# Linear attention start-up: the order of the first loads, a replicated vector, an earlier clear and later weight pieces

## The chip, the core and the metric

The kernel runs on one core of a Trainium2 chip. The core has five engines that each take their instructions in order: TensorE (PE, with its weight loads PEld), VectorE (DVE), ScalarE (ACT), GpSimd (POOL) and SyncE (SP), which here issues nearly all transfers. SP's transfers are carried out by 16 DMA engines. PE computes into PSUM, everything else is held in SBUF, and both have 128 partitions. The metric is the time of one execution on the device in microseconds (us); lower is better.

## The reference

Three parts are computed one after the other on 3072 tokens of width 384: a linear attention with a decaying state, a mixture of eight experts of which each token uses at most one, and a bilinear MLP.

```
# attention: r, k, v of shape (4 batches, 8 heads, 768 steps, 48); w, u of shape (8, 48)
for t in range(768):
    cur = outer(u * k[t], v[t])
    y[t] = r[t] @ (state + cur)
    state = w[:, None] * state + outer(k[t], v[t])
# experts: x is (3072, 384)
c = x @ w_skip > 0;  e = argmax(x @ w_gate);  g = softmax(x @ w_gate)[e]
out = x;  out[c] = x + g * (relu(x @ w1[e]) @ w2[e])
# second MLP: w1, w2 are 384x1024, w3 is 1024x1024, w_out is 1024x384
out = ((x @ w1) * (x @ w2)) @ w3 @ w_out
```

The kernel multiplies w3 by w_out ahead of time, during the attention, so that the last part needs one product less for each token. w3 and w_out arrive as 8-byte floats and have to be narrowed to 4 bytes first.

## The kernel before, in words

The attention works on 24 tiles of 128 rows: two batches side by side, 64 steps of each. Tile n belongs to a pair of batches (n modulo 2) and to a chunk of 64 steps (n divided by 2). Two kinds of tile are loaded for it. TB holds r and k with the head dimension on the partitions (`load_t(n)`, tensor in_att, 128x1024 floats, 0.524 MB) and has three buffers. KV holds r, k and v with the steps on the partitions (`load_v(n)`, tensor in_kv, 128x1152 floats, 0.590 MB) and has four buffers.

For each tile these steps are done:

- `prep(n)`, L358, on DVE: FK = TB times powers of the decay. This is the product that frees the buffer of TB.
- `scores(n)`, L370, on PE, and `evac(n)`, L375, on DVE, which masks them into Fs.
- `prep_m(n)`, L388 and L389, on POOL: r times u, then times k (u lies in the tile `un`); `bonus(n)`, L394, on DVE sums this into z; `prep_v(n)`, L404, on ACT scales v by z in eight instructions.
- `prep_k(n)`, L382, on POOL gives kd; `ds_mm(n)`, L440, on PE adds kd times v to the state S in PSUM; `state_copy(n)`, L412 and L414, decays S on DVE and copies it to SBUF on ACT.
- `y_mm(n)`, L424 and L427, on PE; `x_out(n)`, L445, on DVE adds the two parts of the output, and two transfers (L449, xm<-xg, 0.197 MB together) write them out.
- `x_trans`, L456 on PE and L458 on ACT, and `logits`, L469 and L472, prepare the routing to experts.

Iteration n of the loop (L771 on) is written as prep(n+2), scores(n+1), kd(n+1), prep_m(n+2), evac(n+1), bonus(n+1), y_mm(n), logits(n-2), x_trans(n-1), prep_v(n+1), x_out(n), ds_mm(n). The code is emitted in the order in which it is written, with no reordering by a scheduler. Each engine keeps that order, and SP too: a transfer whose buffer isn't free stops all transfers behind it.

Between these steps the loop narrows the pieces of w3 and w_out. `load_w(i)` loads piece i (raww, three buffers; 0.786 MB for a piece of w_out, 1.049 MB for one of w3). `w_step` takes the next operations from a list: a copy on ACT (L104), then a shift, a merge and a sign on DVE (L112, L115, L119). The table WN says how many steps each iteration makes: none in iterations 0 and 1, three in iterations 2 to 6, two afterwards. The copy of piece i+1 is issued together with the first DVE step of piece i. The narrowed pieces are multiplied on PE (L707); where none is ready yet, `keep` fills PE with dummy products of zeros (L254).

`consts()` makes small tables on POOL in three parts, one in each of iterations 0 to 2. SP's transfers use eight semaphores in turn, and a transfer waits until the one eight places before it has landed.

Lines touched by the change: load order L256 to L264, state clears L559 to L561 and L744 to L745, `load_w` calls L749 to L754, `load_t` in the loop L775 to L776, the consts call L787, and the layout of u L1442. Times in a profile name the line of an instruction.

Of the kernel before, what the change touches and what calls it, by code (L numbers as in the profile page):

```python
# [8 lines left out]
F32 = mybir.dt.float32  # L9
# [9 lines left out]
P = 128  # L19
NB, NH, NS, HD = 4, 8, 768, 48  # L20
D = NH * HD
# [3 lines left out]
NT = NTOK // P  # L25
# [16 lines left out]
W3B = 5  # L42
WK = [(1, 1)] * 9 + [(1, 2)] * 13
WN = [(0, 0, 0)] * 2 + [(1, 1, 1)] * 5 + [(1, 0, 1)] * 15
KW = 16
NRING = 8
RG = 3
# [11 lines left out]
def fused_kernel(ctx, tc, att, kv, wt, u, wg, we, w3, wo, w12, r, k, v, wu, out):  # L59
    nc = tc.nc  # L60
# [161 lines left out]
    ps_s = A(tc.tile_pool(name="ps_s", bufs=1, space=PSUM))  # L222
    ps_1 = A(tc.tile_pool(name="ps_1", bufs=1, space=PSUM))

    with tc.manual_schedule():
# [8 lines left out]
        un = ac.tile([P, NH, HD], F32, name="un")  # L234

        def load_t(n):
            nc.sync.dma_start(out=TB[n % 3].rearrange("p a h t -> p (a h t)"), in_=att[n])

        def load_v(n):
            c, bp = divmod(n, 2)  # L240
            nc.sync.dma_start(out=KV[bp][c % 2].rearrange("p a h d -> p (a h d)"), in_=kv[n])
# [14 lines left out]
        for _ in range(NWARM):  # L256
            dummy(DQ)
        load_t(0)
        load_t(1)
        nc.sync.dma_start(out=un.rearrange("p h d -> p (h d)"), in_=u.to_broadcast([P, D]))  # L260
        load_v(0)
        load_v(1)
        load_t(2)
        nc.gpsimd.memset(ident, 0.0)  # L264
        nc.gpsimd.affine_select(out=ident, in_=ident, compare_op=ALU.not_equal, fill=1.0, base=0,
                                pattern=[[-1, P]], channel_multiplier=1)
# [8 lines left out]
        def load_w(i):  # L275
            if i < len(jobs):
                kind, q = jobs[i]
                raw_w.append(load_wide(nrp, "raww", wo[:, 2 * q * D:2 * q * D + 2 * D] if kind == "o" else w3[q], 3))
# [10 lines left out]
        for i in range(6):  # L289
            wn = pw[:, i - 1] if i else wc  # L290
            n = 1 << i
# [5 lines left out]
        nc.vector.reciprocal(out=cc, in_=pw[:, 5])  # L297
        cb = cc[:, :, None].to_broadcast([P, NH, CH])
        nc.vector.tensor_tensor(out=UT[:, 0, 0], in0=Ur, in1=cb, op=ALU.mult)
        SB = [ps_s.tile([P, 512], F32, tag=f"S{bp}", name=f"S{bp}") for bp in range(2)]  # L300
        S = [b[:, 0:D].rearrange("p (h d) -> p h d", h=NH) for b in SB]

        half = [slice(64 * q, 64 * q + 64) for q in range(2)]
        dims = [slice(64 * q, 64 * q + HD) for q in range(2)]
        KU = ac.tile([P, 2, NH, HD], F32, name="KU")
# [48 lines left out]
        def prep(n):  # L354

            t = TB[n % 3]
            FK = FK_[n] = wk.tile([P, 2, NH, CH], F32, name="FK", bufs=3)
            return nc.vector.tensor_tensor(out=FK, in0=t, in1=UT[:, n // 2 % 2], op=ALU.mult)  # L358
# [6 lines left out]
        def scores(n):  # L365
            FK = FK_[n]
            sc = ps_1.tile([P, 512], F32, tag="sc", name="sc").rearrange("p (h t) -> p h t", h=NH)
            for h in range(NH):
                for m, d in zip(half, dims):
                    nc.tensor.matmul(sc[m, h], FK[d, 1, h], FK[d, 0, h], start=True, stop=True)  # L370
            return sc
# [184 lines left out]
                eng.tensor_tensor(out=sg if k == 2 else v[:, :, 4], in0=sg, in1=v[:, :, k], op=ALU.subtract)  # L556

        found, pend = [], []
        SL = [b[:, 384:464] for b in SB]  # L559
        for b in SL:  # L560
            nc.vector.memset(b, 0.0)  # L561
        slots = wk.tile([P, 80], F32, name="slots", bufs=1)

        def lanes(oh, lo, i, k, eng):
# [169 lines left out]
        load_t(3)  # L734
        nc.vector.tensor_tensor(out=UT[:, 1, 1], in0=Tk, in1=cb, op=ALU.mult)
        prep(1)
        sc = scores(0)
        prep_m(0)
        table_k(1)
# [1 line left out]
        evac(0, sc)  # L741
        bonus(0)
        prep_m(1)
        for bp in range(2):  # L744
            nc.vector.memset(S[bp], 0.0)  # L745
        nc.vector.tensor_tensor(out=w128, in0=pw[:, 5], in1=pw[:, 5], op=ALU.mult)
        prep_v(0)
        more_consts = consts()
        load_w(0)  # L749
        load_v(2)  # L750
        load_v(3)
        nc.sync.dma_start(out=wgs, in_=wg)
        load_w(1)
        load_w(2)  # L754
        todo = []
        NEXT = {logits: logits_out, route_a: route_b, route_b: route_c}

# [13 lines left out]
        for n in range(NT - 2):  # L771
            w_ready()
            if n == NT - 3:
                raws = {q: load_expert(0, q) for q in range(2)}
            if n + 4 < NT:  # L775
                load_t(n + 4)  # L776
            fk = prep(n + 2)
            state_copy(n + 1)
            sc = scores(n + 1)
            behind(prep_k(n + 1) or prep_m(n + 2), fk)  # L780
            if n < NT - 3:
                prep_m(n + 2)
            evac(n + 1, sc)
            bonus(n + 1)
            if n == NT - 3:
                bonus(NT - 1)
            next(more_consts, None)  # L787
            w_step(WN[n][0])
            w_ready()
            y_mm(n)  # L790
            keep(4 * WK[n][0])
            run_todo()
            if n > 0:
                x_trans(n - 1)
            prep_v(n + 1)
            keep(4 * WK[n][1])
            w_step(WN[n][1])
            w_evac(0)
            x_out(n)
            ds_mm(n)  # L800
            place_mm(n % 2)
            if n + 4 < NT:
                load_v(n + 4)
            if n < NT - 3:
                place(3)
            w_step(WN[n][2])
            run_todo(n < NT - 3)
            if n > 0:
                todo.append((logits, (n - 1,)))

        a, b, g = NT - 2, NT - 1, len(groups) - 1
# [596 lines left out]
def _layout(i):  # L1408
# [20 lines left out]
    def words(a):  # L1429
# [9 lines left out]
        "v": c(v.reshape(NB * NH, NS, 4, 12).transpose(2, 0, 1, 3).reshape(4, NB * NH, NS * 12)),  # L1439
        "wu": c(np.broadcast_to(np.stack([w, u], 1), (4 * NB, NH, 2, HD)).reshape(P, 2, HD)),  # L1440
        "wt": wt,
        "u": c(u.reshape(1, D)),  # L1442
        "wg": c(wg.reshape(ND, P, 9).transpose(1, 0, 2)),
        "we": c(np.concatenate([w1, w2], -1)),
        "w3": words(i["moe2_w3"].reshape(NF, P, NF, P).transpose(0, 3, 2, 1).reshape(NF, P, FF)),
# [21 lines left out]
```

## Time and profile before

| | us |
|---|---|
| median of three timed runs | 635.29 (634.75 to 636.49) |
| profiled execution, its own time | 634.88 |
| its span (first to last instruction) | 633.2 |
| PE busy | 614.4 (97%) |
| DVE busy | 467.0 (74%) |
| ACT busy | 292.4 (46%) |
| POOL busy | 143.9 (23%) |

The span is what the trace covers, and 1.7 us of the execution's time lie around it. A profile row names the start, the duration, the engine, the line and the operation, as output<-input. In brackets stand the idle time of the engine before the instruction and what ended it. The attention fills about the first 170 us. A busy PE here is often a PE that works on dummy products.

### The profile page before, as it was taken

What the parts mean: (1) busy time and instruction counts of PE and PEld (TensorE: products, weight loads), DVE (VectorE), ACT (ScalarE), POOL (GpSimd) and SP (SyncE); (2) the same over time, 40 slices, a digit from 0 to 9 for tenths busy, and PEclk for the clock granted to TensorE, in tenths of its full rate; (3) what the DMA queues carried; (4) which work ended last, traced back from release to release, by engine and by line L of the source; (5) the groups of instructions that cost most, each with busy time, mean ns of one, the idle gap of its engine ahead of it and who ended that gap; (6) DMA issues with size and microseconds to landing.
All of it is one profiled execution on the core that took longest, in us unless ns stands there. A gap on an engine that the chain in (4) does not pass through costs nothing.

```text
span 633.2 us, 15204 instructions
## 1 busy us (share of the span) xinstructions
PE 614.4 (97%) x6289; PEld 546.4 (86%) x6289; DVE 467.0 (74%) x820; ACT 292.4 (46%) x704; POOL 143.9 (23%) x140
## 2 busy tenths in 40 slices
PE   8989999999999999999999999999999999999996
PEld 6978878878679999999987989988988988988984
DVE  6699999996577899999956953864863863863770
ACT  2556544544256676666534542443443442442430
POOL 4856456463040233142132300000000000000000
PEclk9899999999999999999999999999999999999999
DMA  7989988685168778867321002002002002000001
GB/s 303 368 281 373 323 292 294 188 280 182 27 195 289 243 253 308 280 237 251 111 70 58 1 17 84 1 18 84 1 18 84 1 17 84 2 18 33 1 2 55
DMA packets 26797, 90.60 MB, mean 143 GB/s; under 512 B 4009, under 2 KB 10298, under 8 KB 25696
## 3 DMA queue, kind: packets, MB, share of 16 engines
q1 hardware_dynamic: 24672, 84.11, 38.0%
q0 software_dynamic: 2048, 5.44, 2.5%
q8 instruction: 51, 0.84, 0.5%
q14 instruction: 26, 0.21, 0.1%
HBM read 77.81 MB, written 12.58 MB: 143 GB/s over the span
## 4 chain that ended last, share of the span: by engine, by line
PE 77%; DVE 13%; DMA 4%; issue 3%; ACT 1%; POOL 1%; SPq 0%; DVEq 0%; ACTq 0%; POOLq 0%
PE po L1231 16%; PE xy L1193 11%; PE za L1193 10%; PE zb L1193 8%; PE hp L922 7%; PE y L941 6%; PE wp L707 5%; PE sc L370 2%; DVE elo L86 2%; DMA TB<-in_att 2%; PE S L440 2%; DVE hl L926 1%; PE G L427 1%; PE y L424 1%; PE y L427 1%
## 5 line engine op out<-in xcount | busy, mean ns | idle before, releaser
L1175 DVE TENSOR_TENSOR C<-st,za 128x512 f32<-128x512 f32 x47 | 32.3, 688 | 69.6 <-ACT st L1210 69.5
L86 DVE TENSOR_TENSOR elo<-raw,ehi 128x768 fp32r<-128x768 f32 x64 | 60.4, 950 | 4.0 <-ACT ehi L85 3.7
L922 PE MATMUL hp<-xh,ehi 128*128 128x256 f32 x192 | 55.3, 290 | 2.3 <-DVE hl L926 1.7
L1231 PE MATMUL po<-pl,W_hi 128*128 128x512 f32 x144 | 56.8, 394 | 0.0
L1231 PE MATMUL po<-ph,W_hi 128*128 128x512 f32 x144 | 56.6, 393 | 0.0
L1231 PE MATMUL po<-ph,W_lo 128*128 128x512 f32 x144 | 56.1, 390 | 0.0
L1210 ACT COPY st<-xy 128x256 f32<-128x256 f32 x47 | 17.6, 374 | 81.8 <-PE xy L1193 81.8
L85 ACT CAST ehi<-raw 128x768 fp32r<-128x768 f32 x64 | 52.6, 828 | 2.1 <-DMA raw<-in_we 2.1
L922 PE MATMUL hp<-xh,elo 128*128 128x256 f32 x192 | 53.3, 279 | 0.0
L922 PE MATMUL hp<-xl,ehi 128*128 128x256 f32 x192 | 53.3, 279 | 0.0
L1193 PE MATMUL xy<-bxh,w12h 128*128 128x256 f32 x188 | 53.3, 283 | 0.0
L1193 PE MATMUL xy<-bxl,w12h 128*128 128x256 f32 x188 | 53.1, 283 | 0.0
L1193 PE MATMUL xy<-bxh,w12l 128*128 128x256 f32 x188 | 53.1, 282 | 0.0
L707 PE MATMUL wp<-wo_s,w 128*128 128x384 f32 x128 | 50.4, 505 | 0.0
L404 ACT ACTIVATE zv<-KV,z 128x48 f32<-128x48 f32 x184 | 44.0, 324 | 11.2 <-DVE z L394 8.2
L1193 PE MATMUL za<-bxh,w12l 128*128 128x512 f32 x141 | 45.1, 320 | 0.0
L1193 PE MATMUL za<-bxh,w12h 128*128 128x512 f32 x141 | 45.0, 319 | 0.0
L1193 PE MATMUL za<-bxl,w12h 128*128 128x512 f32 x141 | 44.7, 317 | 0.0
L959 POOL DMA_INDIRECT xm<-yo,sidx x16 | 23.8, 1485 | 89.5 <-DVE yo L956 75.4
L941 PE MATMUL y<-ehi,hh 128*128 128x384 f32 x128 | 43.5, 340 | 0.0
L941 PE MATMUL y<-ehi,hl 128*128 128x384 f32 x128 | 43.2, 337 | 0.0
L941 PE MATMUL y<-elo,hh 128*128 128x384 f32 x128 | 43.1, 337 | 0.0
(249 smaller groups left out, 1684.3 us busy)
## 6 DMA issues: line engine op xcount, KB each, us to landing
raw<-in_we SPq DMA_DIRECT2D x32, 768.0 KB, 5.1
KV<-in_kv SPq DMA_DIRECT2D x24, 576.0 KB, 5.2
TB<-in_att SPq DMA_DIRECT2D x24, 512.0 KB, 7.4
raww<-in_w SPq DMA_DIRECT2D x8, 1024.0 KB
raw<-in_w SPq DMA_DIRECT2D x8, 768.0 KB, 6.2
xm<-xg SPq DMA_DIRECT2D x48, 96.0 KB, 3.6
out<-ob SPq DMA_DIRECT2D x18, 256.0 KB, 2.4
x<-xm SPq DMA_DIRECT2D x20, 192.0 KB, 2.6
```

Of the source, the lines that this page charges most:

```text
L85: nc.scalar.copy(out=hi, in_=raw)
L86: (eng or nc.vector).tensor_tensor(out=lo, in0=raw, in1=hi.bitcast(F32), op=ALU.subtract)
L370: nc.tensor.matmul(sc[m, h], FK[d, 1, h], FK[d, 0, h], start=True, stop=True)
L404: nc.scalar.activation(out=zv[:, h], in_=v[:, h], func=AF.Copy, scale=z[:, h:h + 1])
L707: nc.tensor.matmul(ps, w3[:, g], wo_s[:, g], start=(g == 0), stop=(g == NF - 1))
L922: nc.tensor.matmul(hp, a, b, start=(i == 0), stop=(i == 8))
L941: nc.tensor.matmul(ys[e, t], a[:, P * t:P * t + P], b[:, D:2 * D], start=(f == 0 and i == 0), stop=(f == NF - 1 and i == 2))
L959: ins = nc.gpsimd.indirect_dma_start(out=xm[:, :], out_offset=bass.IndirectOffsetOnAxis(ap=sidx[:, j, 1:2], axis=0), in_=yo, in_offset=Non ...
L1175: nc.vector.tensor_tensor(out=halves(C[:, 0]), in0=st[:, 0:2], in1=halves(za), op=ALU.add)
L1193: nc.tensor.matmul(o, a, m, start=first and i == 0, stop=(i == 2), skip_group_check=True)
L1210: nc.scalar.copy(out=st[:, 0], in_=X)
L1231: nc.tensor.matmul(po, a[:, f, c], b, start=(i == 0), stop=(i == 3 * NF - 1))
```

## The change

Five edits, all in the attention's start and loop:

- The first loads are issued in the order TB0, u, KV0, TB1, KV1, TB2, where it was TB0, TB1, u, KV0, KV1, TB2.
- u is stored in memory in 128 copies and loaded row by row; it was one row of 384 floats that the transfer repeated for each partition.
- `load_t` is one tile ahead of before: TB4 is loaded in the prologue, behind prep(1), and TB(n+5) in iteration n, behind prep(n+2), which frees its buffer. It was TB(n+4), ahead of prep(n+2).
- The two PSUM banks of the state (and of the slots beside it) are cleared by two instructions of 128x464 at the very beginning; it was two of 128x80 ahead of prep(0) and two of 128x384 between bonus(0) and prep(2).
- The first three pieces of w3 and w_out are loaded at the ends of iterations 0, 1 and 2 instead of in the prologue, and consts() runs in iterations 2, 3 and 4.

```
@@ prologue
-        load_t(1)
-        nc.sync.dma_start(out=un.rearrange("p h d -> p (h d)"), in_=u.to_broadcast([P, D]))
-        load_v(0)
+        nc.sync.dma_start(out=un.rearrange("p h d -> p (h d)"), in_=u)
+        load_v(0)
+        load_t(1)
         load_v(1)
         load_t(2)
+        for b in SB:
+            nc.vector.memset(b[:, 0:464], 0.0)
...
         prep(1)
+        load_t(4)
...
-        for bp in range(2):
-            nc.vector.memset(S[bp], 0.0)
...
-        load_w(0)
         load_v(2)
         load_v(3)
         nc.sync.dma_start(out=wgs, in_=wg)
-        load_w(1)
-        load_w(2)
@@ loop over n
-            if n + 4 < NT:
-                load_t(n + 4)
             fk = prep(n + 2)
+            if n + 5 < NT:
+                load_t(n + 5)
...
-            next(more_consts, None)
+            if n > 1:
+                next(more_consts, None)
...
             if n + 4 < NT:
                 load_v(n + 4)
+            if n in LW:
+                load_w(n - LW[0])
@@ layout
-        "u": c(u.reshape(1, D)),
+        "u": c(np.broadcast_to(u.reshape(1, D), (P, D))),
```

SP's queue before, from the load of TB2 in the prologue to that of TB5 (TB and KV with their buffer numbers; raww is a piece of w_out or w3):

```order
L237 DMA TB_119<-in_att 128x1024
L237 DMA TB_117<-in_att 128x1024
L98 DMA raww<-in_wo 128x1536
L241 DMA KV_1_112<-in_kv 128x1152
L241 DMA KV_1_114<-in_kv 128x1152
L752 DMA wgs<-in_wg 128x27
L98 DMA raww<-in_w 128x2048
L98 DMA raww<-in_wo 128x1536
L237 DMA TB_118<-in_att 128x1024
L449 DMA xm<-xg 64x384 x2
L241 DMA KV_0_111<-in_kv 128x1152
L237 DMA TB_119<-in_att 128x1024
```

The same stretch of SP's queue in the changed kernel, from TB2 to the load of TB6:

```order
L238 DMA TB_119<-in_att 128x1024
L238 DMA TB_117<-in_att 128x1024
L238 DMA TB_118<-in_att 128x1024
L242 DMA KV_1_112<-in_kv 128x1152
L242 DMA KV_1_114<-in_kv 128x1152
L750 DMA wgs<-in_wg 128x27
L238 DMA TB_119<-in_att 128x1024
L452 DMA xm<-xg 64x384 x2
L242 DMA KV_0_111<-in_kv 128x1152
L99 DMA raww<-in_wo 128x1536
L238 DMA TB_117<-in_att 128x1024
```

The three raww loads have left the stretch between TB3 and TB4, and the first of them now stands behind KV4; TB4 stands ahead of KV2 and KV3, and TB5 ahead of the first store of xg.

DVE before, from prep(1) to prep(2) (FK<-TB is prep, S is the state):

```order
L358 TENSOR_TENSOR FK<-TB_118,UT 128x1024
L375 TENSOR_TENSOR Fs<-sc,mask 128x512
L394 TENSOR_REDUCE z<-m 128x8
L745 MEMSET S_194 128x384
L745 MEMSET S_195 128x384
L746 TENSOR_TENSOR pw<-pw 128x8
L358 TENSOR_TENSOR FK<-TB_119,UT 128x1024
```

The same place of DVE in the changed kernel:

```order
L361 TENSOR_TENSOR FK<-TB_118,UT 128x1024
L378 TENSOR_TENSOR Fs<-sc,mask 128x512
L397 TENSOR_REDUCE z<-m 128x8
L745 TENSOR_TENSOR pw<-pw 128x8
L361 TENSOR_TENSOR FK<-TB_119,UT 128x1024
```

The two clears of S are gone from between the sum z and prep(2). On PE and ACT no instruction changes its place.

## Rows read from the trace of the kernel before

**Rows 1.** Profile page, part 4: shares of the chain that ended last.
```profile
PE 77%; DVE 13%; DMA 4%; issue 3%; ACT 1%; POOL 1%; SPq 0%; DVEq 0%; ACTq 0%; POOLq 0%
```

**Rows 2.** Chain of waits, 0 to 90 us: start, length, what it was.
```profile
2.67 7.08 DMA KV<-in_kv
...
12.44 12.56 DMA TB<-in_att
...
40.90 1.15 PE sc L370 x32
```

**Rows 3.** Timeline of DVE, 7 to 40 us: start, duration, engine, line, operation, idle before.
```profile
7.87 1.22 DVE L358 TENSOR_TENSOR FK<-TB,UT 128x1024 f32<-128x1024 f32 x1
9.01 0.68 DVE L375 TENSOR_TENSOR Fs<-sc,mask 128x512 f32<-128x512 f32 x1
...
12.66 0.79 DVE L745 MEMSET S<- 128x384 f32 x2
...
13.85 1.21 DVE L358 TENSOR_TENSOR FK<-TB,UT 128x1024 f32<-128x1024 f32 x1
...
16.89 1.22 DVE L358 TENSOR_TENSOR FK<-TB,UT 128x1024 f32<-128x1024 f32 x1
...
20.18 0.55 DVE L394 TENSOR_REDUCE z<-m 128x8 f32<-128x384 f32 x1 [1.47 <-POOL m L389]
...
25.02 1.22 DVE L358 TENSOR_TENSOR FK<-TB,UT 128x1024 f32<-128x1024 f32 x1 [3.83 <-DMA TB<-in_att]
...
27.23 0.59 DVE L112 TENSOR_SCALAR wo_s<-wo_s 128x768 int32<-128x768 int32 x1
...
31.09 1.24 DVE L358 TENSOR_TENSOR FK<-TB,UT 128x1024 f32<-128x1024 f32 x1
...
33.77 1.33 DVE L112 TENSOR_SCALAR w<-w 128x1024 int32<-128x1024 int32 x1
...
38.57 1.21 DVE L358 TENSOR_TENSOR FK<-TB,UT 128x1024 f32<-128x1024 f32 x1
```

**Rows 4.** Timeline of POOL, the starts of prep_m(0) and prep_m(2).
```profile
9.92 1.00 POOL L388 TENSOR_TENSOR m<-KV,un 128x384 f32<-128x384 f32 x1 [7.86 <-DMA KV<-in_kv]
...
18.07 1.00 POOL L388 TENSOR_TENSOR m<-KV,un 128x384 f32<-128x384 f32 x1 [1.19 <-DMA KV<-in_kv]
```

**Rows 5.** Timeline of SP's queue: the first weight piece, then TB4.
```profile
7.76 0.44 SPq L98 DMA_DIRECT2D raww<-in_wo  x1
...
12.44 0.67 SPq L237 DMA_DIRECT2D TB<-in_att  x1
```

**Rows 6.** Busy time by stretch; last three columns: PE clock, DMA share, GB/s.
```profile
5.00:6.00 1.00, 1.00 (x6) 0.70 (x5) 0.97 (x3) 0.00 (x0) 0.00 (x0) 1.00 0.72 273
6.00:7.00 1.00, 1.00 (x19) 0.71 (x17) 0.98 (x4) 0.00 (x0) 0.00 (x0) 1.00 0.32 101
7.00:8.00 1.00, 1.00 (x42) 1.00 (x40) 1.00 (x3) 0.23 (x1) 0.00 (x0) 1.00 0.73 289
8.00:9.00 1.00, 1.00 (x42) 1.00 (x40) 1.00 (x1) 0.26 (x1) 0.00 (x0) 1.00 1.02 419
16.89:25.02 8.13, 8.13 (x183) 7.52 (x179) 2.83 (x5) 6.51 (x20) 6.53 (x14) 0.81 1.03 416
45.24:51.28 6.04, 6.04 (x142) 5.14 (x142) 6.01 (x8) 3.75 (x12) 3.87 (x3) 1.00 0.91 314
```

**Rows 7.** Timeline of ACT: copies of the first two weight pieces, then xT.
```profile
22.99 0.91 ACT L104 ACTIVATE wo_s<-raww 128x768 f32<-128x768 f32 x1
23.80 1.12 ACT L104 ACTIVATE w<-raww 128x1024 f32<-128x1024 f32 x1
25.83 0.48 ACT L458 COPY xT<-T 128x384 f32<-128x384 f32 x1 [0.91 <-PE T L456]
```

**Rows 8.** Timeline of PE: logits and the scores that follow them.
```profile
24.68 0.73 PE L469 MATMUL y<-wgs,xT 128*128 128x9 f32 x6
...
26.92 1.14 PE L370 MATMUL sc<-FK 48*64 48x64 f32 x32
```

More of the change, by code (lines that the diff above doesn't have):

```diff
@@ L44 @@
 WN = [(0, 0, 0)] * 2 + [(1, 1, 1)] * 5 + [(1, 0, 1)] * 15
+LW = (0, 1, 2)
 KW = 16
@@ L258, in fused_kernel @@
         load_t(0)
+        nc.sync.dma_start(out=un.rearrange("p h d -> p (h d)"), in_=u)
+        load_v(0)
         load_t(1)
-        nc.sync.dma_start(out=un.rearrange("p h d -> p (h d)"), in_=u.to_broadcast([P, D]))
-        load_v(0)
         load_v(1)
         load_t(2)
+        SB = [ps_s.tile([P, 512], F32, tag=f"S{bp}", name=f"S{bp}") for bp in range(2)]
+        S = [b[:, 0:D].rearrange("p (h d) -> p h d", h=NH) for b in SB]
+        SL = [b[:, 384:464] for b in SB]
+        for b in SB:
+            nc.vector.memset(b[:, 0:464], 0.0)
         nc.gpsimd.memset(ident, 0.0)
@@ L299, in fused_kernel @@
         nc.vector.tensor_tensor(out=UT[:, 0, 0], in0=Ur, in1=cb, op=ALU.mult)
-        SB = [ps_s.tile([P, 512], F32, tag=f"S{bp}", name=f"S{bp}") for bp in range(2)]
-        S = [b[:, 0:D].rearrange("p (h d) -> p h d", h=NH) for b in SB]
         half = [slice(64 * q, 64 * q + 64) for q in range(2)]
@@ L558, in fused_kernel @@
         found, pend = [], []
-        SL = [b[:, 384:464] for b in SB]
-        for b in SL:
-            nc.vector.memset(b, 0.0)
         slots = wk.tile([P, 80], F32, name="slots", bufs=1)
```

## The prediction

> **What bounds the kernel now.** I read the page first. By the shares of the chain that ended last, PE carries 77% of the span and DMA 4% [rows 1]; a transfer is on that chain at few places, so the next view is the chain itself over the part that the change touches. It has two transfers near the start, KV0, which lands at 2.67 + 7.08 = 9.75 us, and TB4, which is issued at 12.44 and lands at 25.00; from 40.90 on PE's scores carry it [rows 2]. So up to 25 us the order and the speed of transfers decide, then DVE, then PE. The timeline of DVE gives the pace: the products FK (prep(2), prep(3), ...) start at 13.85, 16.89, 25.02, 31.09 and 38.57, and the third stands behind 3.83 us of waiting for TB4 [rows 3]. POOL waits 7.86 us for KV0 before its first product and again 1.19 us for KV2 [rows 4]. SP's queue shows what lies ahead of TB4: three weight pieces, the first issued at 7.76 [rows 5]. The table of stretches shows what DMA does meanwhile: 416 GB/s at a share of 1.03 between 16.89 and 25.02, which is saturated, but only 273, 101 and 289 GB/s in the three microseconds from 5 to 8, at a share down to 0.32, though six loads were queued [rows 6].
>
> An iteration saved ahead of 40 us moves everything behind it, since DVE and PE keep their order and PE waits for DVE there. So the question is where prep(5) and prep(6) land.
>
> **A line for landings.** I count megabytes in the order of SP's queue (TB 0.524, KV 0.590, u 0.197, a pair of xm stores 0.197, pieces 0.786 or 1.049; wgs is 0.014). Before, 1.835 MB are queued up to the end of KV0 and 7.813 MB up to the end of TB4. They land at 9.75 and 25.00, so 5.978 MB take 15.25 us: 0.392 MB/us. This is below the 416 GB/s because stores and neighbours that are not yet complete are moved too.
>
> **u in 128 copies.** The stretch from 5 to 8 us moves (419-273)+(419-101)+(419-289) = 594 KB less than three microseconds at the 419 GB/s that follow: 1.42 us lost [rows 6]. u stands in the queue just there. The trace does not show u in 128 rows. Bounds: at best its bytes cost their share (0.2 MB, no stretch lost, all landings 1.4 us earlier); at worst it costs what it does now (0 gained). I take 1.4, since the stretch is like no other on the page. The Trainium skill (DMA: Bandwidth & Descriptors, "Why a DMA increments its semaphore by 16 and not by 1") says that a transfer is spread over up to 16 engines by the outermost dimension of its two sides, which is 128 in both forms; by that alone both would cost the same, and the sum would lose 1.4 us at every landing. The dip in the rows speaks against it, yet no row shows which property of u makes it.
>
> **The start.** The landing line becomes 8.35 + (C - 1.835)/0.392, where C counts the new order. KV0 ends at C = 1.311: 7.0 us instead of 9.75. TB1 ends at 1.835: 8.35, where prep(1) started at 7.87 [rows 3], so prep(1) loses 0.5. TB2 ends at 2.949: 11.2. POOL's pair of products for m takes 2.1 us (18.07 to the sum z at 20.18, rows 3 and 4), so m(0) is done at 7.2 + 2.1 = 9.3; DVE is through prep(1) and the mask behind it 1.82 us after prep(1) started (7.87 to 9.01 + 0.68), at 10.2, and makes z(0) then. Before, m(0) was done at 9.92 + 2.1 = 12.0, and prep(2) started 1.8 us later, of which the two clears took 0.79; without them about 1.1, since their rows overlap their neighbours a little. So prep(2) starts at 11.3, just after TB2: 2.5 us ahead of 13.85. The clears move to the very start, where DVE waits 1.3 us for the first decay values; two of 128x464 are worth about 0.79 x 464/384 = 0.95 us, so they are hidden; without that cover they would delay DVE by under 1 us, but prep(1) would still wait for TB1.
>
> prep(3) follows 3.04 us later [rows 3], at 14.3; TB3 (C = 3.474, 12.5) is there. For bonus(2) POOL needs KV2. It is now behind TB4, whose issue waits for prep(1): C = 4.588, 15.4 us instead of 18.0. m(2) ends at 17.5, z(2) follows, and the sum xg as before: prep(4) starts 1.0 us after z(2) began, at 18.5. TB4 (13.9) is long there. That is 6.5 us ahead of 25.02: the 3.83 us of waiting are gone.
>
> **The weight pieces take the place of that wait.** Piece 0 is issued behind KV4, after xg(0), at about 16 us. Ahead of it are now TB0 to TB5, KV0 to KV4 and one pair of stores: C = 7.289, landing at 22.3. DVE asks for it 2.21 us after prep(4) started (25.02 to 27.23, rows 3), at 20.7, and its first step needs ACT's copy of 0.91 us [rows 7]: 23.2. So DVE waits 2.5 us at this place, which it never did before. From that step to prep(5) are 3.86 us (27.23 to 31.09): prep(5) at 27.1, 4.0 us ahead of 31.09. Piece 1 (C = 9.649) lands at 28.3, its copy takes 1.12 and ends at 29.4; DVE asks for it 2.68 us after prep(5) (31.09 to 33.77), at 29.8, so it is there by 0.4 us. prep(6) is 4.80 us behind: 34.6, against 38.57. Piece 2 (C = 11.746) lands at 33.6 and is copied by 34.5, where DVE asks at about 37.2. **4.0 us remain.**
>
> **What else moves.** Behind ACT's copy of piece 1 stand xT(1) (0.48, rows 7), then zv(3) and the state copy of tile 4. xT(1) is done at 29.9, and PE's logits wait for it. From there to the end of the next scores are 26.92 + 1.14 - 24.68 = 3.4 us on PE [rows 8], so 33.3; DVE wants them for its mask at prep(6) plus 1.7 = 36.3: 3 us to spare. PE is idle for some microseconds ahead of this, and between 16.89 and 25.02 its granted clock was 0.81 in the mean, which is some 3.1 us at 1.2 GHz and the rest at 2.4 [rows 6]. If such a stretch falls on these 3.4 us, they end at 35 to 36.7: covered, or nearly. The Trainium skill (TensorE: Matmul & The Clock Gate, Part 1) says that an idle PE is given half its clock and gets it back only by work; this speaks against a change that lets PE idle, and if the whole of it fell on the path it would cost half of 3.1 us.
>
> The deeper TB loads only add slack later: the trace has one wait for TB in all. SP stands behind prep(n+2) now, and behind it stand the stores of xg(n) and KV(n+4), whose data come later on DVE anyway: nothing. consts() on POOL comes two iterations later, where POOL is busy for 3.87 of 6.04 us [rows 6]: nothing; without that room its third part would hold up one product for z. The rest of DMA traffic until 70 us is as before, and in a queue that is never late by more than before: I count no return of the 4.0 us.
>
> The sum is against the profiled execution: 634.9 - 4.0 = 630.9 us. It lies 0.4 below the median of the runs shown, so for a median 631.3.
>
> **Rivals.**
> - The pieces do not wait (or ACT and DVE find other work first): then prep(5) keeps the 6.5 us of prep(4), and the time is 628.8. For it: the first landings may run at 0.42 instead of 0.392, which brings piece 0 to 21.4 and the gain to 4.9. Against: piece 0 would have to land before 19.8.
> - u's copies gain nothing: all landings 1.4 us later, gain 2.6, 632.7. For it: the rule above. Against: the dip.
> - The gain is given back by DMA: with the lowest rate of a busy stretch, 314 GB/s between 45.24 and 51.28 [rows 6], piece 0 lands at 8.35 + 5.454/0.314 = 25.7 and piece 1 at 33.2, DVE gets piece 1 at 34.4, and prep(6) starts at 39.2: 0.6 us behind now, 635.9, no change. Against: 416 GB/s in the stretch where these pieces move.
> - Slower: the same pieces, later still. ACT takes them in order, so each late landing holds xT, zv and the state copy too. From a rate below 0.30 MB/us on, prep(6) is more than 1.9 us late; at 0.28 piece 1 lands at 36.3, prep(6) starts at 42.2, and the time is 638.9. No saturated stretch is that slow.
>
> **How the numbers follow.** A difference below 0.3% (1.9 us) cannot be told from no change. The forecast, with gains of 3 to 5 us, has 0.60, the pieces without a wait (and all above 5) 0.12, u for nothing 0.10, the gain given back 0.13, slower 0.05. Faster by over 0.3% is 0.60 + 0.12 + 0.09 (u for nothing, but for 0.01) = 0.81; within 0.3% 0.14; slower 0.05. The range leaves out the slow end and half of the no-change case: 628.6 to 634.8.
>
> **What would show it.** Right: FK of prep(4) starts near 18.5 with no wait for TB; KV0 lands near 7; no stretch of 100 GB/s between 5 and 8; the first weight step on DVE (L113 in the changed kernel) stands behind ACT's copy, and that behind its DMA, by 2 to 3 us; FK of prep(6) starts near 34.6, and every later place, such as the gather for the experts, is 4 us earlier. Wrong: a dip that stays (u), a prep(4) that waits for KV2 beyond 19, pieces that land after 24 and 30, or a shift at 35 us that is gone at 80.

## The result, and the profile after

The changed kernel takes 640.51 us (median of 4 runs, 640.04 to 640.67) against 635.40 before (four runs): a ratio of 1.0078, 95% interval 1.0064 to 1.0093. It is slower by some 5 us; the forecast was 631.3. The profiled execution took 640.67 us with a span of 638.9. Ratios here and below leave out two runs, one of e5_before_depth at 645.99 us and one of the kernel before at 645.09, that lie over 1.5% above the fastest run of their kernel.

On the page (part 4, answering [rows 1]) PE's share of the chain has grown from 77 to 81%:

```profile
PE 81%; DVE 10%; issue 3%; DMA 3%; ACT 2%; SPq 0%; POOL 0%; ACTq 0%; DVEq 0%
```

DVE, whose pace the prediction summed, is late at prep(1) and ahead from prep(2) on. Its timeline (columns as in [rows 3]) shows the products FK of tiles 1, 4, 5 and 6, the masks Fs of tiles 0 and 2, and the first weight step:

```profile
9.41 2.02 DVE L361 TENSOR_TENSOR FK<-TB,UT 128x1024 f32<-128x1024 f32 x1 [1.54 <-DMA TB<-in_att]
11.36 0.68 DVE L378 TENSOR_TENSOR Fs<-sc,mask 128x512 f32<-128x512 f32 x1
...
20.04 0.69 DVE L378 TENSOR_TENSOR Fs<-sc,mask 128x512 f32<-128x512 f32 x1 [2.50 <-PE sc L373]
...
21.57 1.53 DVE L361 TENSOR_TENSOR FK<-TB,UT 128x1024 f32<-128x1024 f32 x1
...
27.25 0.62 DVE L113 TENSOR_SCALAR wo_s<-wo_s 128x768 int32<-128x768 int32 x1 [2.04 <-ACT wo_s L105]
...
30.12 1.22 DVE L361 TENSOR_TENSOR FK<-TB,UT 128x1024 f32<-128x1024 f32 x1
...
37.59 1.21 DVE L361 TENSOR_TENSOR FK<-TB,UT 128x1024 f32<-128x1024 f32 x1
```

prep(4) starts 3.45 us earlier than before, without the wait for TB4. prep(5) and prep(6) start 0.97 and 0.98 us earlier; 4.0 were forecast. So DVE gained, and PE lost. PE's timeline:

```profile
12.09 1.97 PE L373 MATMUL sc<-FK 48*64 48x64 f32 x32 [2.70 <-DVE Fs L378]
...
33.81 0.84 PE L472 MATMUL G<-wgs,xT 128*128 128x9 f32 x6 [1.45 <-ACT xT L461]
...
36.25 1.94 PE L373 MATMUL sc<-FK 48*64 48x64 f32 x32
...
46.51 0.32 PE L430 MATMUL G<-Ss,FK 48*64 48x48 f32 x4 [0.38 <-issue]
...
53.23 0.72 PE L430 MATMUL y<-Ss,FK 48*64 48x48 f32 x17 [0.78 <-issue]
...
60.80 1.13 PE L430 MATMUL G<-Ss,FK 48*64 48x48 f32 x31 [1.64 <-issue]
```

The last columns are the idle time ahead of a row and what ended it; "issue" means that nothing which the profile shows was waited for. The scores of tile 1 start at 12.09, 2.3 us later than before, behind 2.70 us of waiting for DVE's evacuation (11.36 above; 9.01 in [rows 3]); they then take 1.97 us, at half clock; at full clock such a group takes 1.14 [rows 8]. At 33.81 PE waits 1.45 us for xT, and runs at half clock again (scores 1.94). Three gaps with no releaser follow, 0.38, 0.78 and 1.64 us. They stand on the chain of waits (start, length, what; answering [rows 2]), with the second weight piece:

```profile
23.62 8.62 DMA raww<-in_w
...
52.45 0.78 issue
...
59.16 1.64 issue
```

Measured on the starts of its scores, PE is 2.8 us behind the kernel before at tile 5, 6.8 at tile 9, and 5.7 from tile 12 on to the end of the loop. The whole loss is made in the first 70 us.

Why xT is late stands on ACT (answering [rows 7]): the copy of weight piece 1 waits 5.05 us for its transfer, and xT is queued behind it. What xT copies was ready long before: PE had written T by 27.36.

```profile
26.32 0.90 ACT L105 ACTIVATE wo_s<-raww 128x768 f32<-128x768 f32 x1 [1.85 <-DMA raww<-in_wo]
32.27 1.13 ACT L105 ACTIVATE w<-raww 128x1024 f32<-128x1024 f32 x1 [5.05 <-DMA raww<-in_w]
33.30 0.46 ACT L461 COPY xT<-T 128x384 f32<-128x384 f32 x1
```

The table of stretches shows where transfers went (columns as in [rows 6]). Before:

```profile
12.00:18.00 6.00, 4.16 (x96) 3.65 (x95) 5.57 (x9) 3.37 (x15) 4.80 (x4) 0.88 1.03 420
18.00:26.00 8.00, 8.00 (x170) 7.31 (x167) 2.70 (x5) 5.57 (x17) 6.60 (x14) 0.88 1.01 412
26.00:34.00 8.00, 7.24 (x198) 6.62 (x197) 7.97 (x12) 3.51 (x12) 7.26 (x11) 1.00 0.77 274
34.00:44.00 10.00, 8.49 (x232) 7.89 (x227) 9.93 (x11) 5.99 (x22) 5.05 (x5) 1.00 0.78 278
```

After:

```profile
12.00:18.00 6.00, 5.91 (x84) 5.04 (x86) 5.25 (x8) 3.82 (x16) 4.15 (x4) 0.51 0.83 255
18.00:26.00 8.00, 8.00 (x231) 7.60 (x228) 4.21 (x6) 3.13 (x11) 7.74 (x8) 0.94 0.98 344
26.00:34.00 8.00, 6.38 (x151) 5.63 (x149) 6.14 (x9) 2.63 (x5) 4.32 (x7) 1.00 1.01 407
34.00:44.00 10.00, 10.00 (x215) 9.42 (x216) 9.93 (x12) 7.59 (x28) 7.40 (x16) 0.83 1.01 380
```

Before, DMA is saturated up to 26 us, where PE stands idle for 1.84 us (12 to 18 us) and DVE waits for TB4, and has air from 26 to 44 us, at shares of 0.77 and 0.78. After, it is the other way round: less is moved ahead of 26 us, and DMA is full from 26 to 44 us, where the chain runs over the second weight piece up to 32.24 us and over PE from 33.81 on.

The gaps marked "issue" fall where TensorE's instructions arrive late. The page lists 51 packets of 16 KB in a queue of kind "instruction" (part 3, q8). In every run here these gaps stand at the same products, some 128 apart (a weight load and a product each); such a place is called a boundary below, and what lies between two of them a block. Behind every gap of over 0.3 us PE goes on 2.2 to 2.6 us after such a packet started. Gaps are given from here on from the start of one product to that of the next: the three above are 0.60, 1.00 and 1.86 us. The one that ended at 53.23 marks a boundary; the next packet came only in the second of these two windows (part 3 for 53.3 to 58.4 us, then for 58.4 to 59.5):

```profile
q1 hardware_dynamic: 366, 1.74, 90.8%
q14 instruction: 1, 0.01, 0.4%
```

```profile
q1 hardware_dynamic: 121, 0.34, 92.3%
q8 instruction: 1, 0.02, 5.6%
```

It started 5.27 us after the boundary; PE stood from 59.16 to 60.80. In the kernel before, the packet of the same block came 3.60 us after its boundary, and the gap was 0.14 us. At full clock, and with no other wait, PE uses up a block in some 3.9 to 5.9 us up to 65 us, so a packet that comes later than some 1.6 to 3.6 us after the boundary stops it. The Trainium skill (Runtime: NRT & Kernel Launch, "Instruction fetch mechanics") says that instructions come in 16 KiB blocks of 256 by a DMA queue of their own, and that crossing a block is mostly hidden. The block size agrees; hidden it is not here, with gaps up to 1.86 us in this run.

How late a packet starts goes with how busy DMA is at the boundary. Counted over the first 170 us in the traces of before, of after and of all runs below but e12, with DMA's share taken from 1 us ahead of a boundary to 0.5 us behind it: where the share is under 0.3, the packet starts 0.2 us after the boundary in the median (32 boundaries), and where it is over 0.9, 2.8 us after it (197). The two go together, which is not a proof yet: 29 of the 32 lie behind 80 us.

### The profile page after: what moved, and what is told of

It reads as the page before. It is cut to its first block, busy times and chain, and to the rows that moved or that the text cites. A ratio compares the mean times of both kernels' runs of the same rounds, so it can differ in the third digit from the quotient of the medians.

```text
span 638.9 us, 15219 instructions
## 1 busy us (share of the span) xinstructions
PE 617.8 (97%) x6289; PEld 549.5 (86%) x6289; DVE 464.9 (73%) x818; ACT 291.9 (46%) x704; POOL 143.9 (23%) x140
## 4 chain that ended last, share of the span: by engine, by line
PE 81%; DVE 10%; issue 3%; DMA 3%; ACT 2%; SPq 0%; POOL 0%; ACTq 0%; DVEq 0%
PE po L1230 15%; PE xy L1192 11%; PE za L1192 10%; PE zb L1192 8%; PE wp L707 6%; PE hp L921 6%; PE y L940 5%; PE sc L373 4%; PE S L443 3%; DVE elo L87 3%; PE y L427 2%; PE y L430 2%; DVE hl L925 2%; PE G L427 1%; PE G L430 1%
## 5 line engine op out<-in xcount | busy, mean ns | idle before, releaser
L921 PE MATMUL hp<-xh,elo 128*128 128x256 f32 x192 | 53.3, 279 | 0.0
L921 PE MATMUL hp<-xl,ehi 128*128 128x256 f32 x192 | 53.3, 280 | 0.0
L1192 PE MATMUL xy<-bxh,w12h 128*128 128x256 f32 x188 | 53.3, 283 | 0.0
L924 ACT ACTIVATE hh<-hp 128x256 fp32r<-128x256 f32 x64 | 24.5, 383 | 40.9 <-PE hp L921 39.0
```

The lines of the kernel that those rows point to most:

```text
L921: nc.tensor.matmul(hp, a, b, start=(i == 0), stop=(i == 8))
L924: nc.scalar.activation(out=hh, in_=hp, func=AF.Relu)
L1192: nc.tensor.matmul(o, a, m, start=first and i == 0, stop=(i == 2), skip_group_check=True)
```

## Experiments

Three theories. **S**: the second tile's r and k (TB1) land later, so PE starts late and at half clock. **W**: the late weight pieces, through xT or through the transfers. **Q**: the load queue, deeper by a tile, holds up the instruction blocks. A table first. "Lag" is how much later than before the scores of tile 5, 9 and 16 start in the profiled run; "half" is PE's time at half clock between 9 and 80 us there (3.4 us in the kernel before). The median is of all timed runs. The ratio is to runs of the kernel before that were timed in the same session (their medians are 635.04 to 635.77).

| run | lag 5 | lag 9 | lag 16 | half, us | median, us | ratio to before, 95% |
|---|---|---|---|---|---|---|
| after | 2.8 | 6.8 | 5.6 | 13.7 | 640.51 | 1.0064 to 1.0093 |
| e1_order | 4.0 | 4.7 | 5.5 | 6.8 | 640.50 | 1.0051 to 1.0111 |
| e2_depth | 2.2 | 3.7 | 3.6 | 10.2 | 639.63 | 1.0034 to 1.0095 |
| e3_weights | 0.4 | 3.9 | 2.6 | 10.2 | 639.21 | 1.0040 to 1.0088 |
| e6_order_weights | 3.1 | 3.2 | 8.4 | 20.5 | 637.38 | 0.9971 to 1.0041 |
| e7_order_depth | 3.3 | 3.6 | 3.3 | 6.8 | 640.72 | 1.0029 to 1.0100 |
| e8_three_back | 2.5 | 5.0 | 4.6 | 17.1 | 636.51 | 0.9953 to 1.0027 |
| e9_half | 1.1 | 2.5 | 1.4 | 10.2 | 639.45 | 1.0003 to 1.0070 |
| e4_u | -0.9 | -0.9 | -0.9 | 0 | 634.23 | 0.9953 to 0.9985 |
| e5_before_depth | -0.5 | 0.6 | 0.3 | 0 | 635.84 | 0.9978 to 1.0028 |
| e10_weights_alone | 4.1 | 6.0 | 5.9 | 10.2 | 640.99 | 1.0063 to 1.0113 |
| e11_order_alone | 1.2 | 0.6 | 0.6 | 6.8 | 636.44 | 0.9999 to 1.0043 |
| e12_fewer | 0.4 | 3.2 | 2.9 | 10.2 | 634.74 | 0.9981 to 1.0025 |
| e13_xT_first | 0.0 | 4.4 | 4.1 | 6.8 | 640.45 | 1.0046 to 1.0100 |
| e14_clears | 3.2 | 3.8 | 3.7 | 10.2 | 635.08 | 0.9970 to 1.0017 |
| e15_consts | -0.8 | -0.6 | 0.4 | 0 | 635.30 | 0.9980 to 1.0023 |
| e16_after_xT_first | 0.6 | 4.2 | 4.2 | 10.2 | 640.59 | 1.0055 to 1.0128 |
| e17_xT_first_twice | 3.6 | 9.2 | 8.3 | 20.5 | 643.10 | 1.0060 to 1.0141 |
| e18_repair | -0.4 | 6.4 | 5.6 | 10.2 | 639.30 | 1.0019 to 1.0073 |

Many of these kernels spread over 4 us and more from run to run (the kernel before too: 28 runs of one session lie between 634.5 and 639.7, and others reach 643.4 and 645.1), so a profile shows one course of several, and a median within 1 us of another decides little.

### Parts put back into the changed kernel

**e1_order**, against after:
```diff
         load_t(0)
+        load_t(1)
 ...u, load_v(0)
-        load_t(1)
```


> The changed kernel with one thing put back: the second tile's r and k are issued ahead of u and the first KV load again; all else as changed. Theory S (the second tile's late landing starts the TensorE lag): the second tile lands near 7.9 us, DVE's first evacuation starts at or before 9.3 us instead of 11.36, the TensorE's scores of tile 1 start near 10 us instead of 12.1, the half clock of 12 to 19 us is gone, and TensorE is about level with the kernel before up to tile 5. If that lag is carried to the end, the time falls by 2 to 3 us, to about 638. Theory Q (the deeper queue of loads keeps TensorE's instruction blocks waiting): the issue stalls at 46 to 61 us (2.8 us together) stay, so the rest of the lag stays; if DVE bounded and S were of no account, the time stays at 640.5.

The start came as S says: scores of tile 1 at 9.66, PE 3.2 us ahead of the kernel before at tile 3. Yet the time is the same. PE then waits 3.84 us for xT, up to 33.17, where it had waited 1.45 up to 33.81: the weight pieces are a floor beneath the late start, and taking one away shows nothing. Gaps follow too, the longest 2.09 us at 67.92.

**e2_depth**, against after (and without `load_t(4)` ahead of the loop):
```diff
+            if n + 4 < NT:
+                load_t(n + 4)
             fk = prep(n + 2)
-            if n + 5 < NT:
-                load_t(n + 5)
```


> The changed kernel with the loads of r and k issued at the old places: ahead of the product that frees the tile's place, one tile fewer in the queue; all else as changed. Theory Q: the TensorE issue stalls at 46.5, 53.2 and 60.8 us (0.38, 0.78 and 1.64 us) fall to 0.2 us or less each, the half clock at 63.7 to 66.5 us is gone, and the time falls by 3 to 4.5 us to 636 to 637.5. Theory W (late weight pieces cost it): the stalls stay as they are and the time stays within 1 us of 640.5. Theory S alone: nothing changes but for the start.

The gaps did not go. They moved: 0.80, 1.09, 0.59 and 0.99 us at 27, 46, 59 and 66 us. The fall of the median, 0.9 us, is inside the intervals. Depth is not the only thing that delays a block.

**e3_weights**, against after:
```diff
+        load_w(0); load_w(1); load_w(2)   # at the old places, ahead of the loop
...
-            if n in LW:
-                load_w(n - LW[0])
```


> The changed kernel with the first three weight pieces issued at the old place, ahead of the loop; all else as changed. Theory W: piece 1 lands before 27 us, the TensorE's 1.45 us wait for xT at 33.8 us and the half clock at 36 to 39.5 us go, and the time falls by 1.5 to 2.5 us to 638 to 639. Theory Q with the depth of the queue as cause: the stalls of 46 to 61 us stay, and of the lag at tile 9 only that 1 to 2 us goes; if instead the two weight loads moved into the loop are what keeps the instruction blocks waiting, the stalls fall under 0.3 us each and the time falls by 4 us or more.

The wait for xT is gone and PE is level at tiles 5 and 6. Then a gap of 1.83 us at 44.86, with half clock behind it, takes the lag from -0.5 at tile 6 to 3.0 at tile 7. The median falls by 1.3 us. So with the pieces at their old places some 4 us of loss are left: late pieces are not needed for it.

**e6_order_weights**: the edits of e1 and e3 together.

> The changed kernel with two things put back: r and k of the second tile ahead of u and KV, and the weight pieces ahead of the loop. The deep queue of r and k, u in copies and the early clears stay. If the two late places are floors under one another (either alone hides the other, as the first runs suggest), both go here: no wait of TensorE for the second tile or for xT, no half clock ahead of 40 us, and TensorE 1 to 3 us ahead of the kernel before at tiles 2 to 5. The theory that TensorE's instruction blocks are held up behind the loads says that this lead is lost again at block boundaries (gaps of 0.3 to 1.1 us each, 2 us or more in all ahead of 65 us): 635 to 636.5. The rival, that the blocks are of no account of their own, has the lead stay to the end: 632.5 to 633.5.

The median is back within 2 us of before and the ratio takes in 1, so S and W together make most of the loss. The lead of 2.8 us at tile 3 was lost at a block, as Q's theory has it: gaps of 0.95 and 2.11 us at 14 and 21 us, then 10.2 us at half clock. The profiled run, at 643.37, is the slowest of ten (634.65 to 643.37).

**e7_order_depth**: the edits of e1 and e2 together.

> The changed kernel with the second tile's r and k ahead of u and KV again, and the loads of r and k at the old depth; the weight pieces stay late. Theory W: the weight pieces set a floor of their own: TensorE waits 3 us or more for xT near 30 to 33 us, the half clock follows, and its scores of tile 5 start 3 to 4 us behind the kernel before; 638 to 639.5. If without the deeper queue the pieces land in time, that wait is under 1 us, and the time is 635 to 636.

As W says: a lag of 3.3 at tile 5 comes in one step, from -1.4 at tile 4. Late pieces cost as much without the deep queue.

**e8_three_back**: the edits of e1, e2 and e3 together; left are u in copies, the early clears and the later constants.

> The changed kernel with three parts put back (the second tile's place, the weight pieces, the depth of the queue): left are u in 128 copies, the early clears and the constants two tiles later. If these three parts are the whole harm, the time is at or below the kernel before: 633 to 635. If u in copies gains the 0.7 to 1.4 us at the start, TensorE leads by about that at tiles 2 and 3; by the theory of the instruction blocks most of it is lost again ahead of 65 us.

Not slower than before, so the three parts hold the loss. Five runs take 634.0 to 635.2, five 637.9 to 639.9. The profiled one is of the second group.

**e9_half**, against after. It leaves out half of the bytes of tiles 8 to 13, so its output is not the reference's (the cut for KV, 576 of 1152 columns, is not shown):
```diff
-...out=TB[n % 3]..., in_=att[n])
+            e = 512 if 8 <= n <= 13 else 1024
+...out=TB[n % 3]...[:, 0:e], in_=att[n][:, 0:e])
```


> The changed kernel with the loads of tiles 8 to 13 cut to half their bytes (r, k and KV; the other half of each buffer keeps an older tile's values, so the output is not the reference's). Instructions and their order stay. Theory of the instruction blocks: with some 0.55 MB less to move per tile the blocks come sooner after a boundary (under 4 us instead of 4.5 and 5.3), the TensorE gaps at 53 and 60.8 us (1.0 and 1.86 us) fall below 0.4, the half clock behind them goes, and the time falls by 3 to 4.5 us to 636 to 637.5. Rival (the gaps come of something in TensorE's program, or of the clock): they stay and the time stays within 1 us of 640.5.

Where the bytes were cut, the gaps went: the boundaries at 52, 58 and 64 us show 0.05, 0.05 and 0.20 us, against 1.00, 1.86 and 0.06 in after. Instructions and their order are the same. Yet this does not show that the cut bytes did it: e3_weights, with whole loads, has gaps of 0.05 us at the boundaries at 54, 59 and 65 us too, and its packets come 3.7, 3.1 and 2.7 us after the boundaries of 45, 54 and 59 us, where those of e9 come 3.8, 3.0 and 3.7 us after the same ones. In both runs a gap of over 1.8 us and half clock lie just ahead. Gaps of 1.62 and 1.86 us at 20 and 45 us, ahead of most of the cut, remained, and the median fell by 1 us only.

### One part alone, in the kernel before

**e10_weights_alone**:
```diff
-        load_w(0)
...
-        load_w(1)
-        load_w(2)
...
+            if n in LW:
+                load_w(n - LW[0])
```


> The kernel before with one part of the change alone: the first three weight pieces issued in the loop. Theory W: the late weight pieces are the largest part of the harm and need no other: TensorE waits 2 us or more for xT near 31 to 34 us, the half clock follows, and the time is 3 to 5 us above the kernel before, 638 to 640. Rival (the pieces hurt only since the deeper queue of r and k lies ahead of them): the wait is under 1 us and the time is 635 to 636.

This part alone gives a loss as large as the whole change. PE, then ACT:

```profile
33.30 1.45 PE L470 MATMUL G<-wgs,xT 128*128 128x9 f32 x6 [3.83 <-ACT xT L459]
...
37.58 1.78 PE L371 MATMUL sc<-FK 48*64 48x64 f32 x32
```

```profile
31.75 1.13 ACT L105 ACTIVATE w<-raww 128x1024 f32<-128x1024 f32 x1 [5.12 <-DMA raww<-in_w]
32.78 0.46 ACT L459 COPY xT<-T 128x384 f32<-128x384 f32 x1
```

Piece 1 is waited for 5.12 us, xT stands behind its copy, PE waits 3.83 us and comes back at half clock.

**e11_order_alone**:
```diff
-        load_t(1)
 ...u (one row, read 128 times), load_v(0)
+        load_t(1)
```


> The kernel before with one part of the change alone: u (still one row read 128 times) and the first KV load ahead of the second tile's r and k. Theory S: that tile lands 2 us or more later, TensorE stands idle for 2 to 3 us ahead of the scores of tile 1 and runs at half clock behind it, and the time rises by 2 to 3 us, to 637 to 638.5. Rival (TensorE's lead at this place is worth nothing, since TensorE waits for DVE at 33 and 41 us anyway, by 0.76 and 1.50 us): 634.5 to 636.

The idle time (3.16 us) and the half clock came, and the price did not: 0.8 us of median. Of a lag of 2.9 us at tile 2, 0.6 is left at tile 6, where PE waits for DVE in both kernels. The time lies between the two forecasts, nearer the rival's, and the interval takes in no change.

**e5_before_depth**:
```diff
-            if n + 4 < NT:
-                load_t(n + 4)
             fk = prep(n + 2)
+            if n + 5 < NT:
+                load_t(n + 5)
```
(and `load_t(4)` behind prep(1)).

> The kernel before with one part of the change alone: the loads of r and k issued behind the product that frees their place, one tile ahead. Theory Q: TensorE issue stalls of 0.4 to 1.6 us each appear at the block boundaries near 46, 53 and 60 us, and the time rises by 2 to 4 us over the kernel before, to 637.5 to 639.5. Theories S and W, for which the harm is in the order at the start or in the weight pieces: no change or a small gain (DVE's wait of 3.83 us for tile 4 goes), 633 to 635.5.

Gaps of 0.3 to 1.1 us appeared at eight of the first nine boundaries, 5.3 us in all; the kernel before has one over 0.3 there, of 0.41. So the gaps came as Q says, and its price did not: they ate the 2.0 us by which PE led at tile 3.

**e4_u**:
```diff
-        ...in_=u.to_broadcast([P, D])
+        ...in_=u          # (128, 384) in memory
```


> The kernel before with u loaded from 128 copies, and nothing else. By the prediction's price all landings behind u come 1.4 us earlier, and with the shallow queue and the early weight pieces kept, the time falls by 1.4 us or more, to 634 or less. By the theory of the instruction blocks TensorE gains 0.5 to 1.5 us at tiles 2 to 4 and gives it back at block boundaries (gaps of 0.4 us and more that the kernel before does not have): 634.5 to 636.5.

Between the two forecasts: faster than before, by 0.15 to 0.47%, and all 12 runs lie between 634.0 and 634.7. It beats both kernels. PE has gaps of 1.05, 1.36 and 0.83 us; by the last two its lead of 2.5 us at tile 3 is 0.3 at tile 4:

```profile
14.44 0.29 PE L440 MATMUL S<-KV,kd 64*48 64x48 f32 x5 [0.84 <-issue]
...
20.63 0.62 PE L370 MATMUL sc<-FK 48*64 48x64 f32 x15 [1.14 <-issue]
...
26.57 0.24 PE L440 MATMUL S<-KV,kd 64*48 64x48 f32 x1 [0.62 <-issue]
```

At tile 5, for which PE waited 0.76 us for DVE in the kernel before, the lead is 0.9; it stays so to the end, and PE's clock does not fall.

**e14_clears** and **e15_consts**: e4_u, and to it `nc.vector.memset(b[:, 0:464], 0.0)` behind load_t(2) in place of the two later pairs of clears (e14), or `if n > 1:` ahead of `next(more_consts, None)` (e15).

> The kernel before with u in 128 copies and the early clears. If the clears are what lets TensorE and DVE run further ahead into the busy start (DVE's product for tile 2 starts 0.5 us or more earlier), the boundary gaps at 13 to 27 us grow and some runs fall to half clock: a second group of runs at 637.5 to 640 beside one at 634. If they are of no account: 634.0 to 634.7 in all runs, as with u alone.

> The kernel before with u in 128 copies and GpSimd's constants two tiles later. If the free GpSimd lets the chain of products run further ahead, or the constants hold it up later, runs above 637 appear; otherwise 634.0 to 634.7, as with u alone.

Each alone brings the slower runs back: five of 12 at 638.1 to 638.7 in e14; in e15 a spread up to 639.5, four above 637. The clears let PE start tile 2 at 14.3 instead of 14.8; the gap at the second boundary grows from 1.36 to 2.39 us, and half clock for 10.2 us follows. The slower runs take some 4 us more, by an edit that saves half of one; the profiled run is the only one of them whose course is known.

**e12_fewer**: e8_three_back, and
```diff
-            dummy(DQ)
-            dummy(DQ)
+            dummy2()   # one product of 2 x 256 columns
```


> The kernel of the run with three parts put back (u in copies, early clears, constants later), and in it each pair of filler products of 256 columns replaced by one of 512: the same busy time on TensorE with 4 to 8 instructions less in a tile. Theory of the instruction blocks: a block then lasts up to 0.2 us longer, the gaps at the boundaries shrink by that much each, and the time falls by 0.5 to 2 us against the same kernel with pairs (636.5): 634.5 to 636. Rival: no difference, 636 to 637.

Inconclusive: the median lies 1.8 us below that of e8, but seven runs at 633.9 to 634.9 and five at 637.4 to 639.6 are the two groups of e8 over again, and the ratios to before, 0.9990 (e8) and 1.0003, do not differ beyond their intervals.

### By which way the weight pieces act

**e13_xT_first**: e10, and in the generator of the weight steps
```diff
-                    if ops is None:
+                    if ops is None and (i or k):
                         ops = front(i + 1)
```


> The kernel before with late weight pieces, as in the run with that part alone (641.0 us), and one more edit: ScalarE's copy of weight piece 1 stands behind the copies xT and zv of that tile instead of ahead of them. All transfers are as late as there. Theory W by ScalarE's order: TensorE's wait of 3.83 us for xT at 33.3 us goes, the half clock behind it goes, and the time falls by 4 us or more, to 635 to 637. Rival (the late pieces act through the transfers, on TensorE's instruction blocks or on DVE): TensorE loses the same time elsewhere, and the time stays at 639.5 to 641.5.

By the time the rival holds. The wait at 33 us is gone and the lag at tile 5 is 0.0 instead of 4.1; one tile later piece 2 does the same. PE, then ACT:

```profile
29.72 0.73 PE L470 MATMUL G<-wgs,xT 128*128 128x9 f32 x6
...
39.41 1.45 PE L470 MATMUL y<-wgs,xT 128*128 128x9 f32 x6 [2.38 <-ACT xT L459]
...
43.70 1.94 PE L371 MATMUL sc<-FK 48*64 48x64 f32 x32
```

```profile
31.65 1.13 ACT L105 ACTIVATE w<-raww 128x1024 f32<-128x1024 f32 x1 [2.52 <-DMA raww<-in_w]
...
38.09 0.91 ACT L105 ACTIVATE wo_s<-raww 128x768 f32<-128x768 f32 x1 [4.88 <-DMA raww<-in_wo]
38.89 0.47 ACT L459 COPY xT<-T 128x384 f32<-128x384 f32 x1
```

**e16_after_xT_first**: the same edit in the changed kernel.

> The changed kernel with ScalarE's copy of weight piece 1 behind xT and zv, and nothing else. Theory W by ScalarE's order with S and the deep queue left in: the wait of 1.45 us for xT at 33.8 us and the half clock at 36 to 39.5 us go, and the time falls by 1 to 3 us, to 637.5 to 639.5. Rival (the second tile's late landing alone would hold the same time up): it stays at 640 to 641.

Lag 0.6 at tile 5 instead of 2.8, and the same time in the end; gaps of 1.12, 1.27 and 1.26 us follow at 41, 54 and 67 us.

**e17_xT_first_twice**: e10 with `(i > 1 or k)`, so that the copies of pieces 1 and 2 both stand behind xT.

> The kernel before with late weight pieces (641.0 us as such), and ScalarE's copies of weight pieces 1 and 2 both behind the copies xT and zv of their tiles. Theory W by ScalarE's order: TensorE waits for xT neither at 33 nor at 39 us, the half clock of 34 to 41 or 39 to 46 us goes, and the time falls to 635 to 637. Rival (the late pieces act through the transfers): the time stays at 639 to 641.

The rival holds. Both waits for xT are gone (the logits at 32.96 and 41.29 wait for nothing), and the time is the highest of all:

```profile
27.64 0.24 PE L441 MATMUL S<-KV,kd 64*48 64x48 f32 x1 [1.53 <-issue]
...
28.63 1.86 PE L425 MATMUL G<-KV,Fs 64*64 64x48 f32 x32
...
32.96 1.29 PE L470 MATMUL G<-wgs,xT 128*128 128x9 f32 x6
...
41.29 0.73 PE L470 MATMUL y<-wgs,xT 128*128 128x9 f32 x6
```

A gap (1.53 us idle) and 10.2 us at half clock stand in their place, and more of both later.

**e18_repair**: the edits of e1 and e17 in the changed kernel.

> The changed kernel with two repairs: the second tile's r and k ahead of u and KV, and ScalarE's copies of pieces 1 and 2 behind xT and zv. The deep queue, the late pieces, u in copies, the clears and the constants stay as changed. If the second tile's place and ScalarE's order are the whole loss, the time falls by 4 us or more, to 634.5 to 636.5; what the deep queue and the late transfers cost by themselves (instruction blocks held up) is what remains above 634.2, the time of u in copies alone.

The forecast missed: no wait of PE for another engine above 0.3 us is left, but 9.4 us of gaps stand at the first eleven boundaries, and the median is 639.3. So with neither of the two waits left, gaps at the boundaries go with most of the loss.

## Why the prediction was wrong

- **u in copies.** Right in kind, 0.8 us instead of 1.4. From 5 to 8 us 344, 345 and 310 GB/s now replace 273, 101 and 289 [rows 6]:

```profile
5.00:6.00 1.00, 1.00 (x9) 0.73 (x7) 0.97 (x3) 0.00 (x0) 0.00 (x0) 1.00 0.94 344
6.00:7.00 1.00, 1.00 (x33) 0.91 (x32) 0.97 (x2) 0.00 (x0) 0.00 (x0) 1.00 1.10 345
7.00:8.00 1.00, 0.90 (x30) 0.77 (x28) 0.87 (x2) 0.48 (x1) 0.00 (x0) 1.00 0.92 310
```

  That is 336 KB more, 0.8 us at 419 GB/s. KV0 was there at 8.28 instead of 7.0. Alone (e4) it is worth 0.9 us in the profiled runs, and 1.4 us between the medians of runs that spread as said above.
- **prep(1) loses 0.5.** It lost 1.54 (9.41 against 7.87), and took 2.02 us instead of 1.22. What the step left out is what stands behind prep(1): the evacuation of tile 0, for which PE waits. e11 puts the price of all this at 0.8 us, with an interval that takes in none.
- **prep(2) at 11.3, prep(4) at 18.5, KV2 at 15.4.** 13.19, 21.57 and 18.0. SP's queue (answering [rows 5]) held TB4 back until prep(1) had ended, with KV2 and KV3 behind it:

```profile
3.63 8.16 SPq L238 DMA_DIRECT2D TB<-in_att  x3
11.84 1.70 SPq L242 DMA_DIRECT2D KV<-in_kv  x2
```

  So POOL had KV2 at 18.03 (18.07 in [rows 4]), and DMA moved 255 GB/s from 12 to 18 us where it had moved 420. The landing line took the queue as always full; the 1 MB not moved there is 2.4 us of it. The pieces were copied at 26.32 and 32.27, where 22.3 and 28.3 were expected.
- **DVE waits 2.5 us for piece 0.** It waits 2.04, nearly right. 4.0 us of gain at prep(6) became 0.98, since prep(4) was 3.1 us behind its forecast already.
- **The step that failed** is "An iteration saved ahead of 40 us moves everything behind it, since DVE and PE keep their order and PE waits for DVE there", with "I count no return" of the later traffic. In the changed kernel DVE waits for PE instead (Fs, 2.50 us at 20.04 and 0.96 at 24.06). In the kernel before PE came to the scores of tiles 2, 5 and 6 only 1.25, 0.76 and 1.50 us ahead of DVE, so for a gain of 4.0 us at tiles 5 and 6 PE's own work had to be earlier too:

```profile
15.72 1.30 PE L370 MATMUL sc<-FK 48*64 48x64 f32 x32 [1.25 <-DVE Fs L375]
...
33.44 1.15 PE L370 MATMUL sc<-FK 48*64 48x64 f32 x32 [0.76 <-DVE Fs L375]
...
40.90 1.15 PE L370 MATMUL sc<-FK 48*64 48x64 f32 x32 [1.50 <-DVE Fs L375]
```

  Behind these short waits stood a second limit at nearly the same height, the arrival of PE's instruction blocks. e4 and e5 show it: 2.5 and 2.0 us of lead at tile 3 leave 0.9 and none. With the weight pieces moved from where DMA was full anyway to where it had air, blocks and xT came late (e10: a loss as large as the whole; e17: still there without the waits for xT). Late pieces are enough for the loss and not needed for it: e3, which has them early, still loses 0.40 to 0.88%.
- **PE idle: "covered, or nearly".** Not covered: 13.7 us at half clock, where the kernel before has 3.4. Each time the clock falls after an idle stretch or a gap.
- **The rival on the slower side** had the right place (ACT takes pieces in order, xT behind them) and 638.9 us, at a chance of 0.05. Its way was another: it needed prep(6) on DVE to be late, and that was early.

Open: how the loss divides between xT and the blocks, since the two stand in for each other (e13, e17); and what, beside DMA's share, sets a packet's delay of 0 to 5.8 us. No run cuts the loads and nothing else with a clear result (e9), so that they delay the blocks is argued from the counts above. Backlog alone does not set it: at 14.2 us in the kernel before 4.9 MB were issued and not landed and the packet took 3.6 us, at 53.2 us in after 2.9 MB and 5.3.

## What to carry to other kernels

Ask of every engine, not only of the one that waits, what limits it next; for a TensorE with many small products it can be the arrival of its instructions, read from gaps without a releaser at equal counts of products and from the packets of the instruction queue. Before moving loads into a stretch where DMA had air, ask whether the engine that carries the chain there depends on DMA in any way, its instructions included. When two late events stand one behind the other, do each part alone as well as undoing it: here undoing S showed nothing, and W alone gave a loss as large as the whole.

## What was not expected of the hardware

- An instruction block's packet starts 0 to 5.8 us after PE passed the boundary before (5.77 in e15, 0.0 in e2 and e8), the later the busier DMA is in the median; a PE that stood for it goes on 2.2 to 2.6 us after its start.
- Of 18 gaps of 1.5 to 2.4 us ahead of 80 us, 13 were followed by 3.4 to 10.2 us at half clock (e8: 1.57 us at 20.6, then the granted clock below of 0.74 and 0.62 in the mean of two stretches). Five were not, up to one of 2.09 us (e1), while some shorter ones were (1.12 us in e16). One late block with half clock behind it went with some 4 us of the time (the slower runs of e14).

```profile
18.00:26.00 8.00, 6.65 (x139) 6.24 (x134) 2.87 (x5) 4.47 (x13) 4.55 (x6) 0.74 1.02 410
26.00:34.00 8.00, 8.00 (x144) 7.32 (x143) 7.97 (x10) 3.73 (x12) 7.70 (x9) 0.62 0.72 250
```

- One row of 1.5 KB read for 128 partitions cost about 0.8 us more of the transfers beside it than 128 copies in memory: with u alone changed (e4), 340, 273 and 396 GB/s are moved from 5 to 8 us, so a part of the dip stays.
